# Recurrent attention and a squared-ReLU network: both layers of five token groups in three passes on 12-bit parts instead of fp32 with fewer products

## The chip, the core and the metric

The kernel runs on one core of a Trainium2 chip. The core has a matrix engine (TensorE, "PE" in the profile; its weight loads are "PEld"), a vector engine (VectorE, "DVE"), a scalar engine (ScalarE, "ACT"), GpSimd ("POOL") and SyncE ("SP"), which here issues the DMA transfers. The metric is the device time of one execution in microseconds. Before the change it is 549.76 us, the median of three runs (549.17 to 550.03).

## The reference

```python
for t in range(S):                       # S = 768; batch 4, 8 heads of 48
    state = alpha[:, :, t, :, None] * state + einsum('bhd,bhe->bhde', k[:, :, t], v[:, :, t])
    y[:, :, t] = einsum('bhd,bhde->bhe', q[:, :, t], state)
x = y.transpose(0, 2, 1, 3).reshape(3072, 384)
h = maximum(x @ w_in, 0.0)               # w_in  384 x 2048
out = (h * h) @ w_out                    # w_out 2048 x 384
```

The two weight matrices arrive as float64, the rest as float32. The result is float32.

## The kernel before

**Tiling.** The sequence is cut into 6 chunks of 128 positions. A block is one chunk of one batch element, so there are 24 blocks of 128 tokens; `GB = 4` blocks make a group of 512 tokens, and there are `NG = 6` groups (0 to 5 here and in the code; the change's "two to six" are groups 1 to 5). Attention is computed block by block in chunk form: logarithms of alpha (`ln`), their sums by a triangular matmul (`cs`, L264 and, for blocks from 8 on, L267 and L268 on two fp32r parts), exponentials (`eb`, `ei`), scaled q and k (`mq`, `mk`), transposes (`turn`), their copies to SBUF (`turned_copied`, L540), and then for a pair of blocks `ga` and `gb`: scores (L421), sums for the state (L447), masking (L431), the new state (L458, L466, L467), the outputs y (L397) and their eviction `ev` by 12 copies (L555) into the group's input x. The evicted x has features in partitions and tokens in the free dimension, in three pieces of 128 features.

**Group 0** starts while the weights are still arriving. Each of 16 weight pieces is loaded as raw 64-bit words into one of four `raw` buffers and made into fp32 by `convert_first`, `convert_middle` and `convert_second` (L150 to L179, on VectorE and ScalarE). The layers of group 0 are plain fp32 matmuls: `ffn_in` (L723) and `ffn_out` (L742, with the output copy L752).

**Groups 1 to 5** compute their layers with fewer products. The first layer, `layer_in`, follows the text `LAYER`: each word is a matmul pair (P) on sums of pieces of x and of w_in, or an add, a copy, a ReLU or a square. The matmuls (L674) have 256 columns of fp32; `sum_w_in` makes the sums of w_in once, late in group 0, and `sum_x` those of x once a group. The second layer, `ffn_product` (L780), computes seven products of half matrices where there would be eight, in fp32 matmuls of 192 columns; `sum_w_out` makes the sums of w_out during group 1. Every fp32 matmul shows as two records in the profile.

**Order.** Every engine works its instructions in the order in which the program issues them, and this order is written by hand. `weave(units, events)` issues a list of units of matmul work, each with a cost, and puts every event (a step of attention, a load, a conversion) ahead of the first unit whose summed cost has reached the event's due time. In group 0 all of the units are woven with weight loading, conversion and the first attention blocks. In groups 1 to 4 the first layer runs alone and the second is woven with the attention of the next group's blocks, so that x of the next group is ready when its first layer begins. Group 5 has no attention beside it. All loads and stores stand in the one queue of SyncE. PSUM is divided in two pools of four banks, one for attention (`ps_att`) and one for the layers (`ps_ffn`); the first layer uses both.

## Time and profile before

| | |
|---|---|
| median of three runs | 549.76 us |
| the profiled execution's own time | 549.13 us |
| its span, first to last instruction | 547.4 us |
| TensorE matmul busy | 534.2 us (98%), 5226 records |
| TensorE weight loads busy | 455.3 us (83%) |
| VectorE busy | 368.6 us (67%) |
| ScalarE busy | 235.8 us (43%) |
| granted TensorE clock | 0.998 |
| moved by DMA | 37.02 MB |

The starts of the first matmuls of each stage divide the span:

| group | first layer (us) | second layer, attention woven in (us) |
|---|---|---|
| 1 | 132.80 to 167.33 | 167.33 to 222.80 |
| 2 | 222.80 to 257.33 | 257.33 to 307.68 |
| 3 | 307.68 to 342.2 | 342.2 to 392.34 |
| 4 | 392.34 to 426.87 | 426.87 to 472.28 |
| 5 | 472.28 to 506.81 | 506.81 to 543.22, no attention |

Busy time is the sum of the durations of an engine's records. On VectorE, ScalarE and TensorE neighbouring records overlap: one starts before the one ahead has ended. What a long row of one operation costs is therefore the distance from start to start and not the duration: a 128x512 add (L616) lasts 687 ns, and in a row they start 603 to 609 ns apart; a copy out of PSUM (L698) lasts 586 ns and takes 514; an eviction of y (L555) lasts 365 and takes about 363; a two-operand 128x768 step lasts 957 and takes 875; a ScalarE step of a weight piece (L163, L166) lasts 935 and 905 and takes 836 and 801. L742's records start 323 ns apart, L674's 216, L780's 162.5.

### The profile page before, as it was taken

How to read it: one execution, taken by the hardware profiler on the slowest of the kernel's cores; microseconds unless marked ns; L12 is line 12 of the kernel's file. 1: busy time of each engine (PE TensorE's matmuls, PEld its weight loads, DVE VectorE, ACT ScalarE, POOL GpSimd, SP SyncE). 2: the span in 40 equal slices, each digit the busy share in tenths (PEclk: the TensorE clock that was granted, in tenths of full speed). 3: DMA queues.
4: the chain of work that ended last, by engine and by line, in shares of the span. 5: the costliest groups of instructions: out<-in, count | busy, mean ns of one | idle time of the engine just before them, and what ended most of it. 6: DMA issues, size and time to landing. Idle time of an engine off the chain costs nothing.

```text
span 547.4 us, 12320 instructions
## 1 busy us (share of the span) xinstructions
PE 534.2 (98%) x5226; PEld 455.3 (83%) x5226; DVE 368.6 (67%) x656; ACT 235.8 (43%) x503; POOL 5.9 (1%) x26
## 2 busy tenths in 40 slices
PE   8889999999999999999999999999999999999996
PEld 5654456656889999989999988999988999988996
DVE  4888889993898873778583677673578651577530
ACT  4568874435264354246343236542326440336100
POOL 2010000000000000000000000000000000000000
PEclk9999999999999999999999999999999999999999
DMA  9979577201001664200343300252300000100001
GB/s 162 239 191 278 148 225 204 59 16 57 1 1 30 118 112 88 66 1 0 60 90 63 85 0 1 46 94 55 88 1 0 2 2 2 57 1 0 1 1 57
DMA packets 117085, 37.02 MB, mean 68 GB/s; under 512 B 108820, under 2 KB 111912, under 8 KB 117032
## 3 DMA queue, kind: packets, MB, share of 16 engines
q1 hardware_dynamic: 117032, 36.25, 29.5%
q8 instruction: 41, 0.67, 0.5%
q14 instruction: 12, 0.10, 0.1%
HBM read 31.49 MB, written 4.75 MB: 66 GB/s over the span
## 4 chain that ended last, share of the span: by engine, by line
PE 81%; DVE 10%; ACT 4%; issue 2%; DMA 2%; SPq 0%; POOL 0%; DVEq 0%; POOLq 0%
PE o L780 33%; PE h L674 32%; PE o L742 4%; PE y L397 4%; PE sckv L421 2%; PE T L532 2%; PE sckv L447 2%; ACT power L163 1%; DMA raw<-in_moe_w_in_dram 1%; DVE w_out L176 1%; DMA raw<-in_moe_w_out_dram 1%; DVE power L172 1%; DVE power L150 1%; DVE w_in L176 1%; DVE w_out L179 1%
## 5 line engine op out<-in xcount | busy, mean ns | idle before, releaser
L616 DVE TENSOR_TENSOR hid<-hid,h 128x512 f32<-128x512 f32 x130 | 88.4, 687 | 40.5 <-PE h L674 37.0
L780 PE MATMUL o<-w_out,hid 128*128 128x192 f32 x480 | 82.3, 327 | 0.0
L780 PEld LDWEIGHTS o<-w_out,hid 128*128 128x128 f32 x480 | 78.5, 190 | 0.6
L674 PE MATMUL h<-xs,w_in 128*128 128x256 f32 x320 | 74.8, 379 | 0.0
L555 ACT COPY x<-y 32x256 f32<-32x256 f32 (+2 forms) x132 | 46.3, 365 | 59.7 <-PE y L397 56.1
L674 PEld LDWEIGHTS h<-xs,w_in 128*128 128x128 f32 x320 | 60.7, 190 | 8.3
L674 PE MATMUL h<-x,ws 128*128 128x256 f32 x200 | 49.7, 379 | 0.0
L723 PE MATMUL h<-x,w_in 128*128 128x512 f32 (+1 forms) x108 | 43.5, 550 | 3.3 <-ACT x L555 1.8
L431 DVE COPY_PREDICATED am<-halves_mask,sckv 128x256 f32<-128x256 uint32 x40 | 15.5, 441 | 43.7 <-PE sckv L447 43.7
L698 ACT COPY hid<-h 128x512 f32<-128x512 f32 x20 | 11.7, 586 | 76.7 <-PE h L674 76.7
L780 PE MATMUL o<-t,s 128*128 128x192 f32 x240 | 43.2, 328 | 0.0
L742 PE MATMUL o<-w_out,hid 128*128 128x384 f32 x128 | 42.8, 490 | 0.0
L674 PEld LDWEIGHTS h<-x,ws 128*128 128x128 f32 x200 | 38.0, 190 | 5.2
L674 PE MATMUL h<-x,w_in 128*128 128x256 f32 x160 | 40.2, 379 | 0.0
L780 PEld LDWEIGHTS o<-t,s 128*128 128x128 f32 x240 | 39.5, 190 | 0.3
L723 PEld LDWEIGHTS h<-x,w_in 128*128 128x128 f32 x108 | 20.0, 190 | 23.4 <-issue 16.3
L742 PEld LDWEIGHTS o<-w_out,hid 128*128 128x128 f32 x128 | 23.9, 190 | 16.2 <-issue 0.5
L691 ACT ACTIVATE hid<-hid 128x512 f32<-128x512 f32 x55 | 34.7, 631 | 1.8
L674 PEld LDWEIGHTS h<-x,w_in 128*128 128x128 f32 x160 | 30.4, 190 | 4.1
L674 PE MATMUL h<-xs,ws 128*128 128x256 f32 x120 | 30.0, 379 | 0.0
L694 ACT ACTIVATE hid<-hid 128x512 f32<-128x512 f32 x35 | 22.0, 628 | 16.9 <-DVE hid L616 16.6
L780 PE MATMUL o<-t,hid 128*128 128x192 f32 x160 | 28.8, 331 | 0.0
(128 smaller groups left out, 764.8 us busy)
## 6 DMA issues: line engine op xcount, KB each, us to landing
raw<-in_moe_w_in_dram SPq DMA_DIRECT2D x8, 768.0 KB
raw<-in_moe_w_out_dram SPq DMA_DIRECT2D x8, 768.0 KB
v_in<-in_v_dram SPq DMA_DIRECT2D x24, 192.0 KB
out_dram<-osb SPq DMA_DIRECT2D x24, 192.0 KB
k_in<-in_k_dram SPq DMA_DIRECT2D x23, 192.0 KB
a_in<-in_alpha_dram SPq DMA_DIRECT2D x22, 192.0 KB
q_in<-in_q_dram SPq DMA_DIRECT2D x22, 192.0 KB
last<-row SPq DMA_DIRECT2D x40, 0.8 KB
```

The source lines that it names most:

```text
L176: nc.vector.scalar_tensor_tensor(out=w, in0=upper, scalar=2.0**-20, in1=w, op0=ALU.mult, op1=ALU.add)
L397: ins = nc.tensor.matmul(out=ys[e][64 * half : 64 * half + D + G * e, m % 2, p // 2, t], lhsT=lhsT, rhs=rhs, start=(half, e) not in seen, ...
L431: nc.vector.copy_predicated(out=am_h(n)[:, e, n % 2], data=ps[e][:, 0], mask=halves_mask.bitcast(U32).unsqueeze(1).to_broadcast([128, NP, ...
L555: copy(out=x[to : to + m, kk, t : t + 2], in_=blk[n]["y"][e][r : r + m, :, p // 2],)
L616: nc.vector.tensor_tensor(out=o, in0=x, in1=z, op=op)
L674: nc.tensor.matmul(out=banks[b][:, i, :], lhsT=w_slot(int(w))[:, "uv".index(p), i * 128 : (i + 1) * 128], rhs=x_slot(int(x)), start=(start ...
L691: nc.scalar.activation(out=t, in_=t, func=AF.Square)
L694: nc.scalar.activation(out=part(o), in_=operand(x), func=AF.Relu, scale=1.0 if sign == "+" else -1.0)
L698: nc.scalar.copy(out=part(word[0:2]), in_=operand(word[3:5]))
L723: nc.tensor.matmul(out=ps, lhsT=w[:, kk, c0 : c0 + 128], rhs=xT[g][:, kk, cols], start=(kk == 0), stop=(kk == KM - 1),)
L742: nc.tensor.matmul(out=acc[t][:, 0:DM], lhsT=hid[i][:, j, t * C : (t + 1) * C], rhs=w_out[i][:, j, :], start=(i == 0 and j == 0), stop=(i ...
L780: nc.tensor.matmul(out=acc[k][:, t, :], lhsT=lhs[:, j, t * C : (t + 1) * C], rhs=rhs[:, j, :], start=(first and r == R[0] and j + t == 0), ...
```

## The change

The layers of groups 1 to 5 are computed as they stand (no sums of pieces), but every fp32 product is made of three single passes in fp32r, whose matmuls show as one record each. Each factor is cut into parts of 12 bits: `a` (or `b` for a weight), the rest `l`, and a difference `d` of the two. `in_x` adds six passes (a with b, l with l, three pieces of 128 features each) in a PSUM bank, and ScalarE copies the sum times 2^-12 to SBUF; `in_y` adds three passes (d with d) to the bank, and VectorE adds the two. `in_post` squares: odd units on VectorE in one operation, even ones on ScalarE in two. The second layer does the same with the squares (`split_h`, `diff_h`, `out_x`, `out_y`). A unit is 128 of the 2048 hidden features and all 512 tokens of the group: the first layer's matmuls (L682 after) have 512 columns, the second's (L745 after) 384.

The weights are cut once, by `split_w` and `diff_w`: w_in in the end of group 0, five of the eight pieces of w_out in the first layer of group 1, three in that of group 2 (in group 1 the last three pieces are used in plain fp32: `THIRDS = 5`). The main parts stay in SBUF. The `l` and `d` parts are written to DRAM and read back for every group, in the order of use, by `pump`: it keeps 6 of them in SBUF (9 from group 2's second layer on), and each use issues the next read on SyncE. The pieces share a pool of 25 slots of 3 KB per partition (`wt`), the hidden units one of 22 slots of 2 KB (`two`).

Attention is woven into the first layers instead of the second, with nearly the same due times, and x is cut into its parts (`split_x`, `diff_x`) within the second layer. The first layer uses the four `ps_ffn` banks only. Steps of attention are unchanged; their lines stand some 15 further down.

```diff
+    wt_pool = ctx.enter_context(tc.tile_pool(name="wt", bufs=25))
+    two_pool = ctx.enter_context(tc.tile_pool(name="two", bufs=22))
...
+    E = 2.0**-12
+    NEAR = 1.0 - 2.0**-13
...
+    kept_parts = {
+        (x, w, p): dram.tile([128, NB], FP32, name=f"{x}{w}{p}")
+        for x in "ld" for w in LAYERS for p in range(NW)
+    }
+    here, todo, room = {}, [], [6]
...
+    def split_w(w, p):
+        b = whole[w].pop(p)
+        here["b", w, p] = wt("wb", FP32R, shapes[w])
+        nc.scalar.activation(out=here["b", w, p], in_=b, func=AF.Copy, scale=NEAR)
+        l = here["l", w, p] = wt("wl", FP32R, shapes[w])
+        combine(((l, b, ALU.subtract, here["b", w, p].bitcast(FP32)),))
+        nc.scalar.activation(out=l, in_=l.bitcast(FP32), func=AF.Copy, scale=1.0 / E)
+        nc.sync.dma_start(out=kept_parts["l", w, p], in_=words(l))
+    def diff_w(w, p, stays):
+        b, l = (here[x, w, p].bitcast(FP32) for x in "bl")
+        d = here["d", w, p] = wt("wd", FP32R, shapes[w])
+        combine(((d, b, ALU.subtract, l),))
+        nc.sync.dma_start(out=kept_parts["d", w, p], in_=words(d))
+        if not stays:
+            here.pop(("l", w, p))
+            here.pop(("d", w, p))
+    def pump():
+        while todo and sum(k[0] in "ld" for k in here) < room[0]:
+            key = todo.pop(0)
+            here[key] = wt("w" + key[0], FP32R, shapes[key[1]])
+            nc.sync.dma_start(out=words(here[key]), in_=kept_parts[key])
+    def used(*key):
+        here.pop(key)
+        pump()
+    def split_to(a, l, x):
+        nc.scalar.activation(out=a, in_=x, func=AF.Copy, scale=NEAR)
+        combine(((l, x, ALU.subtract, a.bitcast(FP32)),))
+    def diff_to(d, a, l):
+        nc.vector.scalar_tensor_tensor(
+            out=d, in0=a.bitcast(FP32), scalar=-E, in1=l.bitcast(FP32), op0=ALU.mult, op1=ALU.add
+        )
+    def raw_r(name):
+        return raw_pool.tile([128, KM, GB * C], FP32R, tag="raw", name=name)
+    x_parts = {}
+    def split_x(g):
+        x, x_parts["a"], x_parts["l"] = xT.pop(g), raw_r("xa"), raw_r("xl")
+        for kk in range(KM):
+            split_to(x_parts["a"][:, kk], x_parts["l"][:, kk], x[kk])
+    def diff_x(g):
+        x_parts["d"] = raw_r("xd")
+        for kk in range(KM):
+            diff_to(*(x_parts[k][:, kk] for k in "dal"))
+    def in_passes(j, w, x, start, stop):
+        p, jj = divmod(j, 2)
+        for kk in range(KM):
+            nc.tensor.matmul(
+                out=acc["h", j], lhsT=here[w, "i", p][:, kk, jj * 128 : (jj + 1) * 128],
+                rhs=x_parts[x][:, kk], start=start and kk == 0, stop=stop and kk == KM - 1,
+                skip_group_check=True,
+            )
+        if jj and w != "b":
+            used(w, "i", p)
+    def in_x(j):
+        acc["h", j] = ps_ffn.tile([128, GB * C], FP32, tag="f", name="h")
+        in_passes(j, "b", "a", True, False)
+        in_passes(j, "l", "l", False, True)
+        hid[j] = two_k("hid")
+        nc.scalar.activation(out=hid[j], in_=acc["h", j], func=AF.Copy, scale=E)
+    def in_y(j):
+        in_passes(j, "d", "d", False, True)
+        combine(((hid[j], acc.pop(("h", j)), ALU.add, hid[j]),))
+    def in_post(j):
+        h = hid[j]
+        if j % 2:
+            nc.vector.scalar_tensor_tensor(
+                out=h, in0=h, scalar=0.0, in1=h, op0=ALU.max, op1=ALU.mult
+            )
+        else:
+            nc.scalar.activation(out=h, in_=h, func=AF.Relu)
+            nc.scalar.activation(out=h, in_=h, func=AF.Square)
+    def layer_in(g):
+        units = []
+        for n in range(NJ + 4):
+            if n < NJ:
+                units.append((1.05, in_x, (n,)))
+            if 0 <= n - 2 < NJ:
+                units.append((0.53, in_y, (n - 2,)))
+            if 0 <= n - 3 < NJ:
+                units.append((0, in_post, (n - 3,)))
+            if 12 <= n < 12 + AHEAD:
+                units.append((0, split_h, (n - 12,)))
+                units.append((0, diff_h, (n - 12,)))
+        return units
+    AHEAD, MORE = 3, 4
+    h_parts, h_diff, extra = {}, {}, []
+    def split_h(n):
+        r = n % (AHEAD + MORE)
+        if r < AHEAD:
+            a, l = two_k("ha", FP32R), two_k("hl", FP32R)
+        else:
+            if n < AHEAD + MORE and r == AHEAD:
+                extra[:] = [raw_r("hx") for _ in range(3)]
+            i = 2 * (r - AHEAD)
+            a, l = (extra[i // 3][:, i % 3] for i in (i, i + 1))
+        split_to(a, l, hid.pop(n))
+        h_parts[n] = a, l
+    def diff_h(n):
+        h_diff[n] = two_k("hd", FP32R)
+        diff_to(h_diff[n], *h_parts[n])
+    def of_tile(t, lhs, rhs, start=False, stop=False):
+        nc.tensor.matmul(
+            out=acc[t][:, 0:DM], lhsT=lhs[:, t * C : (t + 1) * C], rhs=rhs,
+            start=start, stop=stop, skip_group_check=True,
+        )
+    def out_x(n, units):
+        p, jj = divmod(n, 2)
+        a, l = h_parts.pop(n)
+        for t in range(GB):
+            if n == 0:
+                acc[t] = ps_ffn.tile([128, GB * C], FP32, tag="f", name="o")
+            of_tile(t, a, here["b", "o", p][:, jj], start=n == 0)
+            of_tile(t, l, here["l", "o", p][:, jj], stop=n == units - 1)
+            if n == units - 1:
+                if t % 2 == 0:
+                    acc["out", t // 2] = cv_pool.tile([128, 2, DM], FP32, tag="upper", name="osb")
+                nc.scalar.activation(
+                    out=acc["out", t // 2][:, t % 2, :], in_=acc[t][:, 0:DM], func=AF.Copy, scale=E
                 )
+        if jj:
+            used("l", "o", p)
+    def out_y(g, ps, last):
+        for t in range(GB):
+            for p in ps:
+                for jj in range(2):
+                    n = 2 * p + jj
+                    lhs, rhs = (h_diff[n], here["d", "o", p]) if n in h_diff else (hid[n], w_out[p])
+                    of_tile(t, lhs, rhs[:, jj], stop=last and (p, jj) == (ps[-1], 1))
+            if last:
+                o = acc["out", t // 2][:, t % 2, :]
+                combine(((o, acc.pop(t)[:, 0:DM], ALU.add, o),))
+                store(g, t, o)
+        for p in ps:
+            for n in (2 * p, 2 * p + 1):
+                (h_diff if n in h_diff else hid).pop(n)
+            if ("d", "o", p) in here:
+                used("d", "o", p)
+    def layer_out(g):
+        done = THIRDS if g == 1 else NW
+        n = 2 * done
+        for i in range(AHEAD, min(n, AHEAD + MORE)):
+            split_h(i)
+            diff_h(i)
+        for i in range(n):
+            out_x(i, n)
+            if i + AHEAD + MORE < n:
+                split_h(i + AHEAD + MORE)
+                diff_h(i + AHEAD + MORE)
+        ps = list(range(done, NW)) + list(range(done))
+        steps = [ps[i : i + 2] for i in range(0, NW, 2)]
+        if g == NG - 1:
+            steps = [ps]
+        for i, pair in enumerate(steps):
+            out_y(g, pair, pair is steps[-1])
+            if g < NG - 1 and i < 2:
+                (split_x, diff_x)[i](g + 1)
+    THIRDS = 5
...
-    events += [(36 + i, sum_w_in, (i,)) for i in range(len(w_sums))]
+    for i, p in enumerate((3, 4, 5, 6, 7, 0, 1, 2)):
+        events += [(36 + 2.5 * i, split_w, ("i", p))]
+        events += [(37.5 + 2.5 * i, diff_w, ("i", p, p < 3))]
     events += attention([(0, GB, False), (18.0, GB + 2, True), (27.5, GB + 4, True, True)], 2.35)
-    events += [(55, sum_x, (1,))]
+    events += [(55.5, split_x, (1,)), (57, diff_x, (1,))]
     weave(units, sorted(events, key=lambda x: x[0]))
+    hid.clear()
+    def stream(g):
+        if g == NG:
+            return
+        keys = [("l", "i", 0)]
+        for p in range(NW):
+            keys += [("l", "i", p + 1), ("d", "i", p)]
+        keys.remove(("l", "i", NW))
+        todo.extend(k for k in keys if g > 1 or k not in here)
+        todo.extend((x, "o", p) for x in "ld" for p in range(THIRDS if g == 1 else NW))
     for g in range(1, NG):
-        between = {}
         if g == 1:
-            between = {3 + 10 * i: lambda i=i: sum_w_out(i) for i in range(2 * NR2)}
-        layer_in(g, between)
+            stream(1)
         events = []
+        if g == 1:
+            fresh = range(THIRDS)
+        elif g == 2:
+            fresh = range(THIRDS, NW)
+        else:
+            fresh = ()
+        for i, p in enumerate(fresh):
+            events += [(1 + 4.5 * i, split_w, ("o", p)), (2.5 + 4.5 * i, diff_w, ("o", p, False))]
         if g + 1 < NG:
             n = GB * (g + 1) + 2
-            pairs = [(0, n, True), (11.5, n + 2, True)]
+            pairs = [(1.2, n, True), (12.5, n + 2, True)]
             if g == 1:
                 pairs = [(0, n - 2, False), (6.8, n, True), (13.4, n + 2, True)]
-            events = attention(pairs, 1) + [(pairs[-1][0] + 11.5, sum_x, (g + 1,))]
-        if g == 1:
-            late = [(0.5 + i, sum_w_out, (2 * NR2 + i,)) for i in range(2 * NR2)]
-            events = sorted(events + late, key=lambda x: x[0])
-        weave([(1, ffn_product, (g, *u)) for u in PARTS], events)
+            events += attention(pairs, 1)
+        events.sort(key=lambda x: x[0])
+        weave(layer_in(g), events)
+        if g > 1:
+            room[0] = 9
+        stream(g + 1)
+        pump()
+        layer_out(g)
```

## The prediction

> **What bounds the kernel now.** I read first the busy line of the page, then TensorE's waits, then the windows between stage borders, then single instructions.
>
> ```profile
> PE 534.2 (98%) x5226; PEld 455.3 (83%) x5226; DVE 368.6 (67%) x656; ACT 235.8 (43%) x503; POOL 5.9 (1%) x26
> ```
>
> TensorE is busy 534.2 of 547.4 us. Its list of waits is headed by
>
> ```profile
> PE h L723 <- ACT x L555: 1.8, 3, 1.3
> PE kT L308 <- DVE k_in L283: 1.3, 1, 1.3
> PE warm L216 <- POOL s L79: 1.1, 1, 1.1
> PE sckv L421 <- DVE us L458: 1.0, 1, 1.0
> ```
>
> and nothing there is over 2 us, so before is a TensorE stream with no holes, and a saved matmul counts in full. The windows (first and second layer of groups 1 and 2, then both of group 5; columns PE, PEld, DVE, ACT, POOL, granted clock, DMA share, GB/s):
>
> ```profile
> 132.80:167.30 34.50, 34.50 (x161) 30.39 (x160) 26.65 (x43) 15.17 (x25) 0.00 (x0) 1.00 0.03 12
> 167.30:222.80 55.50, 55.15 (x973) 52.00 (x973) 39.78 (x89) 25.00 (x70) 0.00 (x0) 1.00 0.51 95
> 222.80:257.30 34.50, 34.50 (x162) 30.39 (x161) 26.34 (x42) 14.56 (x24) 0.00 (x0) 1.00 0.03 12
> 257.30:308.00 50.70, 50.55 (x811) 48.09 (x811) 30.83 (x68) 20.23 (x56) 0.00 (x0) 1.00 0.35 65
> 476.60:511.00 34.40, 34.40 (x167) 30.78 (x167) 25.80 (x39) 14.61 (x24) 0.00 (x0) 1.00 0.00 1
> 511.00:547.40 36.40, 32.21 (x199) 31.92 (x197) 10.12 (x17) 0.98 (x2) 0.00 (x0) 0.97 0.06 22
> ```
>
> The reader should see that ScalarE has half of each layer free and VectorE a quarter of it. By the starts of the first L674 and L780, a first layer lasts 34.5 us (160 records 216 ns apart) and a second without attention 36.4 (224 records 162.5 ns apart). So 55.5, 50.4, 50.1 and 45.4 us of groups 1 to 4 hold 19.1, 14.0, 13.7 and 9.0 of attention.
>
> **What the Trainium skill says.** "TensorE: Matmul & The Clock Gate", section "Back-to-back issue gap", gives N/2.4 + 2.5 ns for one warm pass (isolated): 162.5 at 384 columns, 215.7 at 512. The two-pass fp32 records agree (162.5 for twice 192, 216 for twice 256). The only fp32r matmuls in before do not:
>
> ```profile
> 171.10 0.47 PE L267 MATMUL cs<-hi,causal_r 128*128 128x384 f32 x1
> 171.41 0.34 PE L268 MATMUL cs<-lo,causal_r 128*128 128x384 f32 x1
> 171.59 0.34 PE L267 MATMUL cs<-hi,causal_r 128*128 128x384 f32 x1
> 171.76 0.34 PE L268 MATMUL cs<-lo,causal_r 128*128 128x384 f32 x1
> 171.94 0.97 PE L780 MATMUL o<-t,s 128*128 128x192 f32 x5
> ```
>
> They start 174 to 178 ns apart, 176 in the mean: 16 more than the 160 of streaming. "Perfetto Trace Analysis", section "Tensor Engine Instruction (MATMUL, LD_WEIGHTS)", calls ScalarE and VectorE strict FIFOs and lets TensorE only pull weight loads ahead; the trace agrees so far as TensorE waited 1.0 us at 106.66 for one 0.42 us add (L458) behind VectorE's conversions. "DMA: Bandwidth & Descriptors", section "Specifications", puts HBM at some 358 GB/s for a core; before shows no stream of 3 KB packets alone, but its 3072 B packets took 148 ns, which on 16 engines makes 1.18 us per 384 KB tile, 333 GB/s.
>
> **The change, part by part.**
>
> *TensorE, per group.* In: 160 records of 216 ns go; 16 units of 9 single passes of 512 columns come. No such pass is in the trace. Ends: 216 (the skill) and 235 (176 scaled by 512/384). I take 213.3 + 16 = 230, since the excess looks like a fixed cost: 144 x 0.230 = 33.1, a gain of 1.4 (ends 3.4 and 0.7). Out: 224 x 0.1625 = 36.4 go; 16 x 4 x 3 = 192 passes of 384 columns at 0.176 come, 33.8: a gain of 2.6. Group 1 has 120 of these and 24 plain fp32 matmuls of two records at 0.323 (L742): 21.1 + 15.5 = 36.6, none. Over five groups 5 x 1.4 + 4 x 2.6 - 0.2 = 17.2 us. Attention's own matmuls are unchanged; they only move from the second layer into the first.
>
> *Group 0.* 20 sums of w_in (L616) and 11 of x leave VectorE. In their place come eight splits: ScalarE wb, VectorE wl, ScalarE wl scaled, VectorE wd, with two stores on SP. At 0.84, 0.96, 0.93, 0.96 (rows of L163, L179, L166) one part is about 3.0 us as a chain, and they are set 2.5 units, 3.2 us, apart. What stands there now:
>
> ```profile
> 111.55 0.96 DVE L179 TENSOR_TENSOR w_out<-w_out,power 128x768 f32<-128x768 f32 x1
> ...
> 123.79 4.35 ACT L555 COPY x<-y 32x256 f32<-32x256 f32 x12 [9.64 <-PE y L397]
> 129.13 0.49 ACT L752 ACTIVATE osb<-o 128x384 f32<-128x384 f32 x1 [0.98 <-PE o L742]
> ```
>
> ScalarE's 9.6 us of idle fill up. The eviction of x then starts near 125.8 behind a split, ends at 130, and behind it stand the last split's wb and wl, three xa (0.54) and four output copies. The first pass of group 1 needs a bank that the first output copy frees (about 135.2) and xl (about 136), where before it started at 132.8: +3.
>
> *Group 1, first layer.* TensorE has 33.1 + 19.1 = 52.2. ScalarE gets, at start-to-start times: 16 copies of h 8.2, 13 halves of the even units' squares 7.0, 24 evictions of y 8.7, 24 of kT and qT 6.3, 12 exponentials 4.5, 6 logarithms 2.5, ten weight passes 8.2, three splits of h 1.6, one output copy 0.4: 47.4. VectorE gets 45. Both are below 52, but each is in order and each split makes one wait for the other; following the order of the three queues I find ScalarE blocked some 5.8 us inside the five splits, so 53 of 52. TensorE then waits: 2.4 us for a bank at its fifth unit (the first add is behind hi and lo of attention, which wait for a logarithm behind a split), 1.2 at the eighth, 2.7 for the y banks of the second pair (still being evicted), 4.0 before the last unit (an add behind a wd). Together 10.3. Second layer: out_x(3) waits for split_h(3), behind 12 evictions and the last squares on ScalarE: +2. Some 3 of the late start runs beside these, since the splits go on meanwhile. Groups 0 and 1: 3 + (52.2 + 10.3 + 36.6 + 2 - 90.0) - 3 = about +11.
>
> *Group 2.* Three splits remain; ScalarE 39 of TensorE's 33.1 + 14.0. I find 3 us of stalls in the first layer and 1 in the second: 33.1 + 14.0 + 3 + 33.8 + 1 = 84.9 against 84.9: 0.
>
> *Groups 3, 4, 5.* No splits. 33.1 + 13.7 + 1.6 + 33.8 + 1.2 = 83.4 against 84.6: -1.2. 33.1 + 9.0 + 0.3 + 33.8 + 1.2 = 77.4 against 79.9: -2.5. Group 5 has 33.1 + 33.8 + 0.3 and the same tail of 4.1 us (add and store), 71.3 against 75.1: -3.8. In the second layers VectorE's two operations per unit (1.2 us) and ScalarE's one (0.54) hide under the unit's 1.41; without that cover the split of h would cost 16 x 1.75 a group.
>
> *Transfers.* Per group 32 tiles of 384 KB return from DRAM: 12.6 MB, 38 us of all engines at 1.18, five times. SP issues them in order, each waiting for TensorE to release a slot, and attention's loads stand behind. In group 1's first layer 24 loads (1.05 us each by 192 B packets of 16.4 ns) and 25 tiles make 55 us of some 60: near full. From group 2 on there are 8 us of lead. I cost this at nothing, covered by TensorE's 47 to 52 us; without the cover it is 3 to 10 us, in groups 1 and 2.
>
> *Sum.* 11 + 0 - 1.2 - 2.5 - 3.8 = +3.5 on 547.4: 550.9; 1.7 outside the span makes 552.6; the median shown is 0.6 over the profiled run: 553.2.
>
> **Rivals.**
> *Faster (other side).* The 512-column pass costs 216 ns, as the skill has it. For: fp32 passes of 256 do keep to that formula, and the 16 ns may belong to the short chain of four. Against: four of four showed it. 5 x 144 x 14 ns = 10 us, less where VectorE binds (group 1): -8, so 545. It decides below 225 ns (3.5 us over about 720 passes). Stalls of half my size lead to the same place.
> *Transfers late.* TensorE waits for wl or wd tiles. For: 55 of 60 us, one in-order queue. Against: the tiles have their prefetch slots. +6 to +15: 559 to 568.
> *The gain is real, the stalls in group 1 are not.* Attention and splits slot in, TensorE waits 3 us in all groups: 553 - 13 = 540.
>
> **How the numbers follow.** Mine (net of stalls slower, 549 to 559) .45; the two faster ones .25 and .13; late transfers .10; within 0.2% of before (about what a measurement can tell from no change) .07. Faster .38, same .07, slower .55. The predicted 553.2 has its own range 549 to 559; the range over the cases is 540 to 562, which leaves about .1 on each side.
>
> **What would show it.** Right: L682's starts 225 to 235 ns apart, L745's 176; TensorE idle 8 to 14 us between 135 and 240, put down to DVE and ACT, and group 1 ending near 234 instead of 222.8; groups 3 to 5 shorter by 1 to 4 each. Wrong: 512-column starts near 216; group 1's waits under 5 us; waits on DMA at L682 or L745; ScalarE or VectorE above 95% in groups 3 and 4.

## The result, and the profile after

The changed kernel takes 573.48 us (median of four runs, 572.61 to 576.28) against 549.46 of the kernel before: 1.0445 times as long, with an interval of 1.0406 to 1.0484. The forecast was slower, 553.2 us, with a range up to 562. The sign was right; the loss is 24 us and not 3.4.

The page of the changed kernel, engines' busy time and two of the rows by slice:

```profile
PE 529.5 (93%) x4962; PEld 424.3 (74%) x4962; DVE 377.5 (66%) x635; ACT 323.7 (57%) x664; POOL 5.9 (1%) x26
...
PEclk9999999899998889999899999999999999999999
DMA  9989666365788994069876488765484444698401
```

TensorE, busy 534.2 of 547.4 us before, is now busy 529.5 of 570.8: 41.3 us of idle against 13.2. And the granted clock (the share of its full speed at which TensorE is let run), 9 in all slices before, falls to 8 in five slices between 100 and 285 us. Its mean is 0.982 instead of 0.998, so about 1.8% of 570.8 us is lost to it (10.3 us); the loss before (1.1) falls in the last 2.2 us, after TensorE's last matmul, and costs nothing. How much of it lengthens TensorE's busy time is measured by a run further down (all three left out): the same 4962 matmuls at full clock are busy for 520.3 us, 9.2 less. So the 23.4 us that the span grew are 28.1 more idle and 9.2 for the clock, less 13.9 of TensorE's work that really went.

TensorE's list of waits after (waited for, us in total, times, longest):

```profile
PE h L682 <- DVE hid L625: 10.3, 6, 2.8
PE sckv L436 <- DVE us L473: 3.7, 1, 3.7
PE o L745 <- DVE hid L625: 3.3, 6, 1.2
PE y L412 <- DVE us L473: 2.6, 1, 2.6
PE h L682 <- ACT osb L841: 2.3, 1, 2.3
...
PE sckv L436 <- issue: 1.7, 1, 1.7
PE o L745 <- ACT hx L656: 1.6, 2, 1.1
```

None is on a weight part; most of the time is spent on VectorE. The windows of the end of group 0, of group 1, group 2 and the first layer of group 3 (stretch and length in us; busy us and instructions of PE, PEld, DVE, ACT and POOL; granted clock, DMA share, GB/s):

```profile
92.00:139.70 47.70, 41.52 (x485) 25.46 (x483) 32.99 (x47) 30.88 (x60) 0.00 (x0) 0.96 0.53 166
139.70:209.50 69.80, 58.97 (x892) 46.34 (x893) 50.64 (x97) 49.43 (x113) 0.00 (x0) 0.90 0.87 227
209.50:246.00 36.50, 36.50 (x169) 29.95 (x168) 16.18 (x26) 9.12 (x18) 0.00 (x0) 1.00 0.29 100
246.00:299.70 53.70, 49.33 (x730) 39.59 (x729) 35.45 (x67) 35.41 (x78) 0.00 (x0) 0.97 0.87 234
299.70:336.20 36.50, 34.48 (x193) 33.13 (x193) 26.39 (x43) 17.00 (x36) 0.00 (x0) 1.00 0.61 200
336.20:385.30 49.10, 46.67 (x699) 38.14 (x697) 29.51 (x60) 31.30 (x72) 0.00 (x0) 1.00 0.78 206
```

By the first matmul of each stage, in us ("forecast" repeats the sums of the prediction):

| stage | before | forecast | after |
|---|---|---|---|
| group 0 | 132.8 | 135.8 | 139.7 |
| group 1, first and second layer | 34.5 + 55.5 | 59.5 + 38.6 | 69.9 + 36.5 |
| group 2 | 34.5 + 50.4 | 50.1 + 34.8 | 53.7 + 36.5 |
| group 3 | 34.5 + 50.1 | 48.4 + 35.0 | 49.1 + 36.3 |
| group 4 | 34.5 + 45.4 | 42.4 + 35.0 | 41.9 + 35.9 |
| group 5 with the tail | 34.5 + 40.6 | 33.4 + 37.9 | 33.9 + 37.5 |

From group 3 on the forecast holds within 2 us a group. The loss is made between 92 and 336 us, in groups 0 to 2.

Of the clock one stretch is enough to see what happens. TensorE after, in group 1's first layer (start, us, instruction, idle before it):

```profile
152.23 0.85 PE L682 MATMUL h<-xd,wd 128*128 128x512 f32 x3
155.17 1.65 PE L682 MATMUL h<-xa,wb 128*128 128x512 f32 x3 [2.08 <-DVE hid L625]
156.61 1.48 PE L682 MATMUL h<-xl,wl 128*128 128x512 f32 x3
157.89 0.52 PE L282 MATMUL cs<-hi,causal_r 128*128 128x384 f32 x1
```

After a wait of 2.08 us three passes take 1.44 and 1.28 us from row to row, where three took 0.69 ahead of it: half the rate, for 3.4 us. The same follows the waits that end at 109.45, 177.61, 196.56, 205.58 (1.7 us) and, a little later, 276.98: six times in all.

### The profile page after: what moved, and what is told of

It reads as the page before. It is cut to its first block, busy times and chain, and to the rows that moved or that the text cites. A ratio compares the mean times of both kernels' runs of the same rounds, so it can differ in the third digit from the quotient of the medians.

```text
span 570.8 us, 12354 instructions
## 1 busy us (share of the span) xinstructions
PE 529.5 (93%) x4962; PEld 424.3 (74%) x4962; DVE 377.5 (66%) x635; ACT 323.7 (57%) x664; POOL 5.9 (1%) x26
## 4 chain that ended last, share of the span: by engine, by line
PE 59%; ACT 15%; DVE 14%; DMA 6%; issue 4%; SPq 2%; DVEq 0%; ACTq 0%
PE o L745 27%; PE h L682 22%; ACT x L574 4%; PE h L811 2%; PE y L412 2%; DVE wl L625 2%; DMA v_in<-in_v_dram 2%; ACT wl L633 1%; PE T L547 1%; DVE hid L625 1%; DMA row<-b 1%; DMA raw<-in_moe_w_in_dram 1%; DMA a_in<-in_alpha_dram 1%; ACT power L180 1%; ACT hid L708 1%
## 5 line engine op out<-in xcount | busy, mean ns | idle before, releaser
L625 DVE TENSOR_TENSOR hid<-h,hid 128x512 f32<-128x512 f32 x80 | 54.7, 687 | 43.7 <-PE h L682 38.8
L682 PE MATMUL h<-xa,wb 128*128 128x512 f32 x240 | 71.4, 407 | 12.6 <-DVE hid L625 10.3
L682 PE MATMUL h<-xd,wd 128*128 128x512 f32 x240 | 71.2, 411 | 1.1 <-ACT hid L695 1.1
L682 PE MATMUL h<-xl,wl 128*128 128x512 f32 x240 | 69.9, 401 | 0.0
L682 PEld LDWEIGHTS h<-xa,wb 128*128 128x128 f32 x240 | 45.2, 193 | 25.3 <-DVE hid L625 13.1
L745 PE MATMUL o<-wb,ha 128*128 128x384 f32 x152 | 51.9, 341 | 3.3 <-DVE hid L625 3.3
L682 PEld LDWEIGHTS h<-xl,wl 128*128 128x128 f32 x240 | 46.4, 193 | 10.4
L745 PE MATMUL o<-wd,hd 128*128 128x384 f32 x296 | 53.8, 338 | 0.0
L682 PEld LDWEIGHTS h<-xd,wd 128*128 128x128 f32 x240 | 44.4, 193 | 11.0 <-ACT hid L695 1.9
L745 PEld LDWEIGHTS o<-wd,hd 128*128 128x128 f32 x296 | 51.5, 188 | 1.1
L745 PE MATMUL o<-wl,hl 128*128 128x384 f32 x152 | 50.9, 335 | 0.0
L745 PE MATMUL o<-wb,hx 128*128 128x384 f32 x144 | 48.5, 337 | 1.6 <-ACT hx L656 1.6
L745 PE MATMUL o<-wl,hx 128*128 128x384 f32 x144 | 48.6, 337 | 0.8 <-DVE hx L625 0.8
L625 DVE TENSOR_TENSOR osb<-o,osb 128x384 f32<-128x384 f32 x20 | 11.2, 558 | 42.0 <-PE o L745 40.4
L811 PEld LDWEIGHTS h<-x,w_in 128*128 128x128 f32 x108 | 20.0, 190 | 23.4 <-issue 16.3
L831 PEld LDWEIGHTS o<-w_out,hid 128*128 128x128 f32 x128 | 24.7, 196 | 17.0 <-issue 1.9
L745 PEld LDWEIGHTS o<-wb,ha 128*128 128x128 f32 x152 | 28.7, 189 | 6.2 <-DVE hid L625 5.8
```

Source lines behind the costliest of these rows:

```text
L625: nc.vector.tensor_tensor(out=o, in0=x, in1=z, op=op)
L682: nc.tensor.matmul(out=acc["h", j], lhsT=here[w, "i", p][:, kk, jj * 128 : (jj + 1) * 128], rhs=x_parts[x][:, kk], start=start and kk == 0 ...
L745: nc.tensor.matmul(out=acc[t][:, 0:DM], lhsT=lhs[:, t * C : (t + 1) * C], rhs=rhs, start=start, stop=stop, skip_group_check=True,)
L811: nc.tensor.matmul(out=ps, lhsT=w[:, kk, c0 : c0 + 128], rhs=xT[g][kk][:, cols], start=(kk == 0), stop=(kk == KM - 1),)
L831: nc.tensor.matmul(out=acc[t][:, 0:DM], lhsT=hid[per * i + j][:, t * C : (t + 1) * C], rhs=w_out[i][:, j, :], start=(i == 0 and j == 0), s ...
```

## The experiments

The expectations weigh two accounts. Theory Q blames the queues of ScalarE and VectorE, which work in order, and the clock that drops after long waits; theory T blames transfers that come late. The edits are shown shortened; words in angle brackets and comments stand for code.

**Do the reads from DRAM cost?** The chain of work that ended last, followed through groups 1 and 2, holds three transfers of attention (start, us, what):

```profile
149.94 3.43 DMA row<-b
...
185.94 3.91 DMA v_in<-in_v_dram
...
266.05 4.61 DMA last<-row
```

```diff
 def pump():
...
-            here[key] = wt("w" + key[0], FP32R, shapes[key[1]])
-            nc.sync.dma_start(out=words(here[key]), in_=kept_parts[key])
+            here[key] = <the resident part l or d of piece 0 of w_in>
```

> The changed kernel without its 148 reads of weight parts from DRAM: every use of an l or d part of a weight takes one resident part, so the output is not the reference's; all other work, the stores of the parts among it, stays. Theory Q (the first layers of groups 1 and 2 lose their time to the in-order queues of ScalarE and VectorE, and TensorE's clock drops after the longer stalls): 569 to 574 us, since the splits and evictions are untouched; TensorE's waits as they were. Theory T (the reads delay attention's loads, rows and stores of the state, which stand in the chain with 3.4, 3.9 and 4.6 us pieces in groups 1 and 2): those pieces go, and with them 8 to 14 us: 558 to 565.

567.06 us (565.5 to 568.62), 6.4 less than with the reads. Group 1's first layer takes 64.8 (69.9), group 2's 50.2 (53.7), group 3's 48.0 (49.1); of the three transfers one row of 2.46 us is left in the chain. So it lies below what theory Q and above what theory T gave: the reads cost about a quarter of the loss and can't be the whole. In group 1's first layer TensorE waits 2.0 us less (8.8 for 10.8); the other 3 us are a better clock there (0.95 for 0.90), which by the run on waits below is in part chance. Whether the small transfers are late because the reads stand ahead of them in SyncE's queue or because the transfer engines are full (0.87 of group 1's first layer) was not tried.

**Do the splits of w_out?**

```diff
         for i, p in enumerate(fresh):
-            events += [(1 + 4.5 * i, split_w, ("o", p)), (2.5 + 4.5 * i, diff_w, ("o", p, False))]
+            here["b", "o", p] = <part b of piece p of w_in>    # l and d likewise, from w_in's in DRAM
```

> The changed kernel without the eight splits of w_out in the first layers of groups 1 and 2 (16 ScalarE, 16 VectorE steps of 128x768 and 16 stores less): the second layer takes the parts of w_in in their place, so the output is not the reference's. Theory Q: group 1's first layer falls from 69.8 us by 8 to 12 and group 2's from 53.7 by 2 to 5: 556 to 564 us. Theory T (late transfers): only the 16 stores go: 568 to 573.

558.13 us (557.2 to 559.07), 15.3 less. Group 1's first layer falls from 69.9 to 59.6 and group 2's from 53.7 to 48.7: inside what theory Q gave for each. Of group 1's 10.3 us, 7.3 are waits of TensorE (3.5 are left) and 2.9 its busy time, at a clock of 0.94 for 0.90. The 16 stores of the parts go with the splits and were not left out alone.

**And those of w_in?**

```diff
-    for i, p in enumerate((3, 4, 5, 6, 7, 0, 1, 2)):
-        events += [(36 + 2.5 * i, split_w, ("i", p))]
-        events += [(37.5 + 2.5 * i, diff_w, ("i", p, p < 3))]
+    events += [(48.5, split_w, ("i", 0)), (50, diff_w, ("i", 0, True))]   # used for all eight
```

> The changed kernel with one split of w_in in group 0 instead of eight: groups 1 to 5 take that one part everywhere, so the output is not the reference's. Theory Q: the 3.7 us wait at 109 us and most of the late start of the first layer go, group 1 begins near 134 instead of 139.7, 566 to 570 us. Rival: the end of group 0 is late by the eviction of x and its parts alone, as the splits only fill idle time of ScalarE: group 1 begins at 138 or later, 571 to 574.

564.07 us (563.17 to 564.97), 9.4 less. Group 1 begins at 131.1 us, not at 139.7. That is 1.7 earlier than in the kernel before, so the seven splits left out, with their 14 stores, account for more than the whole delay. The time is below the 566 to 570 that theory Q gave.

**All three left out.** The edits of the last three runs together.

> The changed kernel without any of the three: one split of w_in, none of w_out, no reads of parts from DRAM (output not the reference's). Left are the three-pass matmuls, the splits of x and h and attention in the first layers. If the three causes add, 573.5 less 6.4 (reads), 15.3 (splits of w_out) and what the run with one split of w_in gives: 545 to 549. If they overlap (a stall has several causes and goes only with the last of them), less than their sum: 550 to 556.

546.31 us (546.1 to 546.52), 0.9938 of the kernel before (0.9918 to 0.9958). The three single effects, 6.4 + 15.3 + 9.4 = 31.1, come to 27.2 together: they nearly add. The page and the window of group 1's first layer of this run:

```profile
PE 520.3 (96%) x4962; PEld 418.3 (77%) x4962; DVE 350.8 (64%) x605; ACT 301.4 (55%) x634; POOL 5.9 (1%) x26
```

```profile
131.80:188.10 56.30, 52.85 (x894) 42.44 (x893) 38.05 (x80) 40.14 (x98) 0.00 (x0) 1.00 0.48 91
```

This is the clearest line of the study. The same matmuls keep TensorE busy for 52.85 us at a clock of 1.00, where the changed kernel takes 58.97 at 0.90; the prediction had 52.2. And 520.3 us of busy TensorE is 13.9 less than before. So the three-pass layers with attention in the first do save, but even with the weight parts neither made nor moved (those of x and h still are) only 0.6%; the kernel pays 27 us to make and move the weight parts. The first layer has only the four `ps_ffn` banks here too, and TensorE still waits no more than 3.5 us in it.

**What does a wait of TensorE cost by itself?**

```diff
+    def gap(copies):                # woven into group 5's second layer of the kernel before
+        nc.tensor.matmul(out=one, lhsT=s[:, 0:128], rhs=s_t[0], start=True, stop=True)
+        nc.scalar.copy(out=t, in_=one)
+        for _ in range(copies):     # 0, 2, 4, 6, 9, 13
+            nc.scalar.copy(out=t, in_=t)
+        nc.tensor.matmul(out=two, lhsT=s[:, 0:128], rhs=t, start=True, stop=True)
```

> The kernel before, with six chains in the second layer of group 5 that make TensorE wait: a matmul, its copy by ScalarE, 0, 2, 4, 6, 9 and 13 further copies, and a matmul on the result; about 1 to 5 us each, some 17 us in all. If a wait costs only itself, L780's records stay 162.5 ns apart right after each and the time is 549.5 plus the sum of the waits. If the clock drops after long waits, records after the ones of over 2 us are some 325 apart for about 3 us, and each of these costs about 1.6 us more than its length, 5 to 8 us in all.

One run, 579.28 us. TensorE in three of the six places:

```profile
527.58 0.70 PE L914 MATMUL gap<-am,s 128*128 128x256 f32 x2 [2.26 <-ACT am L913]
528.12 1.46 PE L780 MATMUL o<-t,ws 128*128 128x192 f32 x8
...
537.05 1.13 PE L914 MATMUL gap<-am,s 128*128 128x256 f32 x2 [3.13 <-ACT am L913]
537.97 6.66 PE L780 MATMUL o<-w_out,hid 128*128 128x192 f32 x32
...
564.48 1.22 PE L914 MATMUL gap<-am,s 128*128 128x256 f32 x2 [6.18 <-ACT am L913]
565.50 2.65 PE L780 MATMUL o<-t,hid 128*128 128x192 f32 x8
```

After 0.52, 1.39 and 2.26 us of waiting L780 goes on at its 162.5 ns (eight in 1.30). After 3.13 the next matmul lasts 1.13 us instead of 0.70 and 32 records of L780 take 6.49 us to the next row instead of 5.2, and after 6.18 eight take 2.48: 1.7 us or a little more lost behind each, on top of the wait. The sum agrees: 18.2 us of waits, 6.5 for the twelve matmuls of the chains (0.54 each from row to row) and 1.7, 2.2 and 1.7 for the clock make 30.3; 29.9 were measured. The second account of the expectation holds, though not for every wait of over 2 us: that of 2.26 cost only itself.

The page "TensorE: Matmul & The Clock Gate" of the Trainium skill, section "Part 1: The HAM clock gate (the "warmup" mystery)", says that TensorE runs at half clock after an idle window of about 3.4 us and for as long again until it is busy, with free-running windows. The runs agree on the half rate and the 3.4 us. They differ on the wait that is needed: 2.08 us was enough, 2.31 at 139.70 and 2.26 in the last run were not. The granted clock in narrow windows shows why. In the changed kernel it is one half in six stretches of 3.41 us, which start at 110.83, 155.20, 179.09, 196.16, 206.40 and 278.08 us: all whole multiples of 3.413 us apart. So, as the page has it, the time is cut on a fixed grid, and not from the start of a wait. The windows of this grid around the waits of 2.31 and 2.08 us in the changed kernel (columns as above):

```profile
134.72:138.14 3.42, 2.68 (x9) 1.26 (x7) 1.49 (x2) 2.37 (x5) 0.00 (x0) 1.00 0.00 0
138.14:141.55 3.41, 1.85 (x8) 1.54 (x9) 3.41 (x7) 3.39 (x9) 0.00 (x0) 1.00 0.91 339
151.79:155.20 3.41, 1.33 (x7) 0.77 (x5) 1.85 (x5) 3.13 (x9) 0.00 (x0) 1.00 0.95 334
155.20:158.61 3.41, 3.41 (x9) 2.84 (x10) 2.81 (x5) 2.85 (x8) 0.00 (x0) 0.50 0.86 172
```

and, in the run with the chains, around those of 2.26 and 3.13:

```profile
523.52:526.93 3.41, 1.80 (x11) 1.40 (x9) 0.61 (x2) 1.42 (x4) 0.00 (x0) 1.00 0.00 0
533.76:537.17 3.41, 0.28 (x2) 0.12 (x2) 0.00 (x0) 2.80 (x7) 0.00 (x0) 1.00 0.00 0
537.17:540.58 3.41, 3.41 (x11) 3.23 (x12) 0.00 (x0) 0.00 (x0) 0.00 (x0) 0.50 0.02 5
```

The waits of 2.31 and 2.26 us are cut by an edge of the grid, so that no window has more than 1.6 us of idle; those of 2.08 and 3.13 lie in one window, and the next runs at half clock. Over the traces of all fourteen kernels of this study, 38 windows at full clock had 1.95 us or more of idle TensorE, and all 38 were followed by half clock; of 64 with 1.28 to 1.82 us 18 were, and of the 2086 with less none. A reader of the page would take the window to be idle throughout; here 1.95 of its 3.41 us were enough. What decides between 1.28 and 1.82 us stays open.

**Is it the back-and-forth between two engines?** The timelines of ScalarE and VectorE after, at the end of group 0, show each split waiting twice:

```profile
122.15 0.83 ACT L630 ACTIVATE wb<-w_in 128x768 fp32r<-128x768 f32 x1
124.14 0.84 ACT L633 ACTIVATE wl<-wl 128x768 fp32r<-128x768 f32 x1 [1.16 <-DVE wl L625]
```

```profile
123.16 0.95 DVE L625 TENSOR_TENSOR wl<-w_in,wb 128x768 fp32r<-128x768 f32 x1
125.02 0.96 DVE L625 TENSOR_TENSOR wd<-wb,wl 128x768 fp32r<-128x768 f32 x1 [0.91 <-ACT wl L633]
```

```diff
-        combine(((l, b, ALU.subtract, here["b", w, p].bitcast(FP32)),))
-        nc.scalar.activation(out=l, in_=l.bitcast(FP32), func=AF.Copy, scale=1.0 / E)
+        nc.scalar.activation(out=l, in_=b, func=AF.Copy, scale=NEAR / E)
+        nc.vector.scalar_tensor_tensor(
+            out=l, in0=b, scalar=1.0 / E, in1=l.bitcast(FP32), op0=ALU.mult, op1=ALU.subtract)
```

> The changed kernel with the same number of split steps in the same places, but one-way: ScalarE makes wb and then the scaled rounded weight, VectorE takes it from the scaled weight in one step and makes wd; ScalarE no longer waits for VectorE within a split. Nothing is left out and the values are the same. If the back-and-forth is what costs (ScalarE idle 1.0 to 1.2 us in each of 16 splits, 16 to 18 us, and VectorE idle 0.9 in most): group 0 3 to 6 us, group 1's first layer 4 to 8, group 2's 1 to 3 shorter: 556 to 565 us. If it is the amount of work in the queues: 569 to 574.

571.06 us (568.83 to 572.57): 2.4 less, with overlapping ranges, and within the 569 to 574 set down for the amount of work. Group 1 still begins at 139.5 and its first layer takes 69.7. The waits inside the splits are gone and ScalarE stands idle for 4.7 us ahead of the last eviction instead. So the interlock, on which the prediction had built its 5.8 us of blocked ScalarE, is not the cause.

**Is it where the splits stand?**

```diff
-        events += [(36 + 2.5 * i, split_w, ("i", p))]
-        events += [(37.5 + 2.5 * i, diff_w, ("i", p, p < 3))]
+        events += [(43 + 1.2 * i, split_w, ("i", p))]
+        events += [(43.9 + 1.2 * i, diff_w, ("i", p, p < 3))]
```

> The one-way splits, and in group 0 their due times moved from 36 + 2.5i to 43 + 1.2i: after the conversions of the weights and ahead of the last eviction of x. Nothing else. If the splits of w_in cost because of where they stand in the queues of ScalarE and VectorE (the 4.8 us wait at 110 us is behind them, and the last one stands behind the eviction), group 1 begins at 132 to 135 instead of 139.5 and the time is 563 to 567 us. If their amount is what costs, group 1 begins at 138 or later: 569 to 573.

565.68 us (565.58 to 565.78), 7.8 less than the changed kernel and 5.4 less than with the one-way splits alone. Group 1 begins at 133.5. Against the 131.1 of the run with one split, the same work costs group 0 8.4 us at the old due times and 2.4 at the new ones, after the conversions of the weights and ahead of the last eviction. TensorE's wait at 109.45 is gone. In group 1, where nothing was moved, the first layer still takes 68.3 us.

**Other places for the work.** Three versions that compute everything were slower than the change itself. First, attention back in the second layers:

```diff
-            pairs = [(1.2, n, True), (12.5, n + 2, True)]
+            pairs = [(0, n, True), (11.5, n + 2, True)]
...
-            events += attention(pairs, 1)
+            later = attention(pairs, 1)
...
-        layer_out(g)
+        weave(layer_out(g), later)          # attention, then split_x, diff_x
```

> The changed kernel with attention woven into the second layers again, at the due times of the kernel before; the splits of w_out stay alone in the first layers. Theory Q: ScalarE's and VectorE's work is spread over both layers, the stalls of groups 1 and 2 go but for a few us and the three-pass layers show their gain: group 0 stays 7 us over before, groups 1 to 5 fall 4 to 5 each below before except group 1 with 0 to 3: 533 to 547 us. Theory T: transfers per group are the same and attention's are still queued with them: 560 to 573. A third, that the three-pass layers themselves cost what they seem to save: 555 to 565.

587.03 us (586.26 to 590.25). The first layers are short (39.4 us in group 1, 34 to 36 after), but the second take 62.7, 56.3, 57.2 and 52.9. Two of TensorE's waits in it:

```profile
PE T L547 <- DVE k_in L298: 12.4, 4, 3.3
PE h L682 <- DVE osb L625: 9.6, 5, 3.2
```

VectorE begins each second layer with four splits of h, and k's scaling stands behind them; at its end the output adds stand behind the splits of x. Every account failed here (the highest gave 573), theory Q with its 533 to 547 first of all: spreading the work by engine totals is no use when the first thing that TensorE needs is last in a queue.

Then half of attention in each layer, three splits of w_in and three of w_out in group 1's first layer:

```diff
+                events += attention([(5, n, True)], 1.6)
+                later = attention([(3, n + 2, True)], 1.2)
...
+                events += [(8.5 + 3.2 * i, split_w, ("i", p)), (10 + 3.2 * i, diff_w, ("i", p, True))]
...
-    THIRDS = 5
+    THIRDS = 3
```

> A version meant to keep the three-pass layers and lose the stalls: attention of a group's first pair woven in the first layer and of its second pair in the second, three of the eight splits of w_in moved into the first layer of group 1, in which three parts of w_out are split (kept in SBUF for that group), five in group 2's; six plain fp32 units more in group 1's second layer. Theory Q: group 1 begins near 136, groups 2 to 4 last 80 to 83 us each, 543 to 553 us. If the transfers or the queues of ScalarE and VectorE still bind, 555 to 570.

588.85 us (587.41 to 591.04). Group 1 begins at 134.9, as hoped, and its layers take 48.4 + 58.0, group 2's 47.8 + 48.5; the first of its waits are on ScalarE's copies of h (9.2 us) and of the outputs (7.4). Both ranges set down (543 to 553 and 555 to 570) were missed. It shows only that this order is no better.

Then three steps of each split on GpSimd:

```diff
-        combine(((l, b, ALU.subtract, here["b", w, p].bitcast(FP32)),))
-        nc.scalar.activation(out=l, in_=l.bitcast(FP32), func=AF.Copy, scale=1.0 / E)
+        nc.gpsimd.tensor_tensor(
+            out=l, in0=b, in1=here["b", w, p].bitcast(FP32), op=ALU.subtract)
+        nc.gpsimd.tensor_scalar(
+            out=l, in0=l.bitcast(FP32), scalar1=1.0 / E, scalar2=None, op0=ALU.mult)
...
-        combine(((d, b, ALU.subtract, l),))
+        nc.gpsimd.tensor_tensor(out=d, in0=b, in1=l, op=ALU.subtract)
```

> The changed kernel with three of the four steps of each weight split (wl, its scaling, wd) on GpSimd, which is otherwise idle, instead of VectorE, ScalarE and VectorE; wb stays on ScalarE. Nothing is left out. Theory Q (the splits cost by making the in-order queues of ScalarE and VectorE wait for each other): with the chain in a queue of its own, group 0 ends 4 to 7 us earlier, group 1's first layer is 6 to 11 us and group 2's 2 to 4 us shorter: 552 to 561 us. Rival: GpSimd is so slow over 128x768 (no such row in the traces) that the parts come late, or it slows VectorE beside it: TensorE waits for wl or wd in the first layers, 570 us or more.

590.34 us (587.2 to 592.05). The rows of GpSimd, and one of TensorE's waits:

```profile
L634 POOL TENSOR_SCALAR wl<-wl 128x768 fp32r<-128x768 f32 x16 | 36.2, 2264 | 1.4
L641 POOL TENSOR_TENSOR wd<-wb,wl 128x768 fp32r<-128x768 f32 x16 | 30.0, 1878 | 1.7 <-DMA do<-wd 0.4
```

```profile
PE y L412 <- POOLq L517: 11.2, 2, 5.8
```

A split is 6 us there, over the 3.2 us between two of them in group 0, which ends at 150.7. And `ga` passes its order for the outputs y through GpSimd (the `passed` instruction), which now stands behind the splits for 11.2 us. The rival was right, with an addition that it didn't have.

**A repair.** One-way, retimed splits of w_in; group 1's second layer in plain fp32, with all eight splits of w_out woven into it; two splits of h ahead of the last squares:

```diff
+        if g == 1:                           # layer_out of group 1
+            for p in range(NW):
+                for t in range(GB):
+                    ffn_out(g, t, p)
+                if p in (2, 4):
+                    (split_x, diff_x)[p // 2 - 1](g + 1)
+                split_w("o", p)
+                diff_w("o", p, False)
...
+            if g > 1 and n in (17, 18):      # layer_in
+                units.append((0, split_h, (n - 14,)))
+                units.append((0, diff_h, (n - 14,)))
```

> An attempt at the repair, with nothing left out: the retimed one-way splits of w_in, group 1's second layer in plain fp32 with all eight splits of w_out woven into it (ScalarE and VectorE have little else there), no split of w_out in any first layer, and the splits of units 3 and 4 of h ahead of the last squares. From the runs before: group 0 134, group 1 59.6 + 41.5, group 2 48.7 + 35, group 3 47.8 + 35, group 4 42 + 34.8, group 5 33.9 + 36.5: a span of 549, 545 to 556 us. If the causes overlap or new waits come up at the moved work: 558 to 568.

551.95 us (548.81 to 555.15 in 16 runs), 1.0049 of before (1.0030 to 1.0067): within the 545 to 556 expected. Group 1 takes 58.6 + 41.0 us, group 2 49.4 + 36.2, group 3 47.8 + 36.0, group 4 42.0 + 35.6: the first layers as the runs before had them, the second of groups 2 to 4 about 1 us over what was expected. ScalarE at the end of group 0 in this run:

```profile
127.00 0.83 ACT L632 ACTIVATE wl<-w_in 128x768 fp32r<-128x768 f32 x1
127.85 4.36 ACT L574 COPY x<-y 32x256 f32<-32x256 f32 x12
132.23 1.67 ACT L657 ACTIVATE xa<-x 128x512 fp32r<-128x512 f32 x3
```

The eviction's y was there at 122.9. One split was therefore put behind it:

```diff
-    for i, p in enumerate((3, 4, 5, 6, 7, 0, 1, 2)):
+    for i, p in enumerate((3, 4, 5, 6, 7, 0, 1)):
...
+    events += [(58, split_w, ("i", 2)), (58.5, diff_w, ("i", 2, True))]
```

> The repair with one split of w_in (piece 2, first used by group 1's fifth unit) moved behind the eviction of x and its parts. In the repair ScalarE began that eviction at 127.85 us though y was there at 122.9, with three splits ahead; TensorE then waited 2.35 us at 134.47 and ran some 3.5 us at a lower clock. If that wait goes, the lower clock goes with it: 3 to 5 us, 547 to 549 us, within 0.4% of before. If the splits ahead still hold the eviction, 550 to 552.

550.85 us (548.82 to 554.64 in 22 runs), 1.0031 of before (1.0020 to 1.0042). Group 1 begins at 132.0 instead of 134.5, and the profiled clock is 0.997. That is 1.1 of the 3 to 5 us expected, and the intervals of the two repairs overlap. The kernel before remains the fastest that does the whole computation.

## Why the prediction was right or wrong

*TensorE's passes: right.* Forecast 230 and 176 ns; in steady rows L682 starts every 227 ns and L745 every 173. The rival of 216 ns is out:

```profile
520.56 0.84 PE L682 MATMUL h<-xa,wb 128*128 128x512 f32 x3
521.24 0.84 PE L682 MATMUL h<-xl,wl 128*128 128x512 f32 x3
```

Three passes in 0.68 us, from row to row. The saving is 13.9 us of busy time against the 17.2 forecast. At the steady rates it would have been more than forecast (5 x 1.9 + 4 x 3.2 = 22). What is missing is in part a first pass of about 335 ns after other matmuls or a wait (at 139.70 and 167.45) where the next take 231 to 235: with all three left out, the 720 passes of 512 columns take 171.7 us and not the 165.6 of the forecast, and 43 of them follow other work or a wait, at 0.31 us in the mean. The prediction's own lines have it: the first of its four passes starts 0.31 us ahead of the next, the others 0.17 to 0.18; it went by the others alone. The 16 ns over streaming, on the other hand, are 13 and 14, and fixed as assumed.

*Group 1's stalls: right in size, for a partly wrong reason, and without their second price.* Forecast 10.3 us of waits; the window shows 69.80 - 58.97 = 10.8 idle. Four waits stand much as in the walk: 2.1, 0.9, 2.6 and 2.7 us (at 155.17, 167.45, 177.61 and 196.56) for 2.4, 1.2, 2.7 and 4.0, the first two at a later unit and the third on VectorE's `us` and not on banks being evicted. That the sum agrees is in part luck: 2.0 of the 10.8 go with the reads, which were put at nothing.

The step that failed is the next: TensorE's matmuls were summed at the full clock. Each of the six stretches at half clock loses 1.7 us: four in group 1's first layer, one in group 0, one in group 2, together 10.2. Of this, 9.2 us show as longer busy time (529.5 for 520.3). That is almost half of the 20 us by which the forecast span fell short (550.9 for 570.8); 7.4 are more idle than forecast (41.3 for 33.9), and 3.3 the saving that was smaller. The 3 us by which the late start was to overlap the stalls did not come either. The interlock within a split, given as the reason, was answered by the one-way splits: it is not the cause. What the work is that stands ahead of a needed step, and where, is: leaving out the splits of w_out took 10.3 us from this layer, and retiming those of w_in 6.0 from group 0; with the splits of w_out moved to the second layer, in the repair, the first takes 58.6.

*Group 0: mis-sized.* +3 was forecast from the eviction at its end, +6.9 came. The 3.7 us wait for `us` (a step of attention's state) at 109.45, behind a split and a conversion on VectorE, was not in the walk, which began at the eviction. It is 2.7 longer than before, and with the 1.7 of its slow clock it makes the last y complete 4.4 us later (128.16 for 123.73). The walk's own part, 2.0 us of eviction held behind a split, came as 2.3. Its sum of one split is off: the four steps make 3.7 us and not 3.0, and took 3.8 (122.15 to 125.98); but the next one starts before the last step, so one began every 2.74 us.

*Transfers "at nothing": wrong.* The cover named, TensorE's 47 to 52 us a layer, hides the parts themselves, and no wait is on them. But attention's rows and loads stand in the same queue and were late: 6.4 us go with the reads, inside the 3 to 10 that the prediction gave for lost cover and should have put in the sum.

*Groups 2 to 5.* Group 2 +5.3 for 0: 1.7 is the clock; 3.5 of its first layer go with the reads and 5.0 with the splits of w_out, which overlap. Groups 3, 4 and 5: +0.8, -2.1 and -3.7, forecast -1.2, -2.5 and -3.8. Groups 2 to 4 lose 1 to 2 us at the start of the second layer to the splits of h (L745 waits for `hid` and `hx`), more than the 1.2 set down. The prediction's two windows of group 5 begin 4 us late (the stage starts at 472.28); its sums go by the starts and are not touched.

*The range.* The range ended at 562, since each case had one cause; the case of late transfers alone had been given up to 568. Here the case of stalls, that of late transfers and an unnamed one, the clock, came together.

## What to carry to other kernels

A wait of the matmul engine of some 2 us or more can cost its length and 1.7 us on top: price stalls one by one, and read the clock of each window. When a cheaper form of the main work needs prepared operands, ask first what the change is worth with the preparation left out; here that run gave 0.6% (3 us), against 27 us of preparation. And totals by engine say little where queues are in order: the same splits of w_in cost group 0 8.4 us or 2.4 by where they stand.

## What was not expected of the hardware

- A single fp32r pass with 384 columns starts 173 ns after the one ahead and one with 512 columns 227, where two-pass fp32 records of the same streamed columns keep to 162.5 and 216: 11 ns more a pass, the same for both lengths.
- The clock halved after waits of 1.7 and 2.08 us and not after 2.31 in another place of the same run: what counted was the idle within one window of a fixed 3.41 us grid, and 1.95 us of it was always enough. The four runs of the changed kernel spread over 3.7 us with clocks of 0.975 to 0.985, those of the kernel before over 1.0 us.
- GpSimd took 1.88 to 2.00 us for a two-operand fp32 step over 128x768 and 2.26 us for one with a single operand, against 0.96 on VectorE for two operands.
